# A batch-norm convolution kernel: rows of the transformed input padded from 342 to 344 columns, and both short blocks kept in one tile

## The chip, the cores and the metric

One core of a Trainium2 chip runs the whole kernel. The metric is the device time of one execution in microseconds (us), lower is better. The time before is 182.66 us, the median of three runs (182.33 to 183.10). One execution was profiled; its own time is 182.38 us.

## The reference: what is computed

`x` is 2 x 2048 x 1024 (item, position, input channel), `w` is 3 x 1024 x 1024 (tap, input channel, output channel), all bf16. A convolution over positions with three taps is followed by batch norm and SiLU:

```python
xp = jnp.pad(x, ((0, 0), (1, 1), (0, 0)))
y = sum(jnp.einsum('bsc,cd->bsd', xp[:, k:k + S, :], w[k]) for k in range(3))
y = (y - mean) * (g * 1.0 / jnp.sqrt(var + 1e-5)) + b
return silu(y)
```

## The kernel before, in words

The convolution is done in the Winograd manner: six neighbouring outputs are made from eight transformed inputs (`NJ = 8` points, `R = 6`). The 2048 positions of an item make 342 tiles of six (`NTILES`). A column tile is 128 input channels (`CT = 8`), an output tile 128 output channels (`DC = 8`).

**Input transform (the first 36 us).** A window holds 128 positions and gives 21 tiles (`WT`). For each item `bi` and column tile `ct` there are 16 windows. One matmul per window (line 225) multiplies it with a small matrix `rm` and leaves 8 x 21 = 168 values per channel in PSUM. A *job* (`Jobs.do`, line 220) is up to six such matmuls into two PSUM banks and one copy ("cast", line 240, executed at 242 on ScalarE, `a`, or 244 on VectorE, `d`) that writes them as bf16 into `T_sb[bi][:, ct, :, f*WT:...]`: 8 rows (one per point), in each a run of 126 or 84 columns. Three jobs (6, 6 and 4 windows; 128x1008, 128x1008 and 128x672 elements) fill a column tile. The last 6 of the 342 tiles of each item come from a *short block* (`do_short`, line 229): 48 rows of x, eight matmuls of 48 columns (line 233) and one cast that writes 6 columns into all 64 rows of `T_sb[bi]`. So `T_sb[bi]` is 128 partitions x 8 column tiles x 8 points x 342 columns.

**The order** is written by hand for every engine. `ORDER` (line 28) lists it: a letter names the pair of PSUM banks of a job (A: 4 and 5, B: 6 and 7, C: 2 and 3, D: 0 and 1), the small letter behind it the engine of the cast, `s2d` and `s4d` are the two short blocks, `z5` five idle matmuls, a number so many matmuls of the first product unit (`First`, line 391), which runs between the jobs. The framework adds the waits between engines: a reader waits for its writer, and an instruction that writes a place waits for whatever it sees as touching the same place before. PE, VectorE (DVE) and ScalarE (ACT) each work strictly in their order.

**Loads.** Everything is loaded by the SP queue in program order (lines 515 to 529), two half tiles by the ACT queue. The x tiles have six buffers (`XBUFS`), so from the seventh on a load waits until PE is done with an earlier one. `load_small` (line 88) takes the one buffer of `xlpool`, twice in turn.

**Products.** A product unit (output tile `dc`, item `bi`) runs eight products, one per point j; each is eight matmuls over the column tiles, with `T_sb[bi][:, ct, j, :]` (342 columns) as the moving operand (line 272; 391 for the first unit, whose item is 0). VectorE and ScalarE combine the eight results into six outputs and apply SiLU; POOL prepares the transformed weights of later output tiles. The last unit is cut into two halves of 214 and 128 columns (`Half`).

The lines that the change touches: 72 (allocation of `T_sb`), 86 to 91 (`load_small`), 229 to 238 (`do_short`).

Of the kernel before, what the change touches and what calls it, by code (L numbers as in the profile page):

```python
# [10 lines left out]
BF16 = mybir.dt.bfloat16  # L11
ENG = mybir.EngineType

P = 128
R = 6
NJ = 8
WT = 21
XBUFS = 6
LROWS = 48
NTILES = 342  # L20
NBP = 384


# [11 lines left out]
def kernel(  # L35
# [9 lines left out]
    nc = tc.nc  # L45
    B, CT, _, NF, _ = x.shape
    DC = w.shape[0]
    NB = NTILES
    LAST = NB - NF * WT
# [4 lines left out]
    tpool = ctx.enter_context(tc.tile_pool(name="tpool", bufs=1))  # L54
# [10 lines left out]
    xlpool = xscope.enter_context(tc.tile_pool(name="xlpool", bufs=1))  # L65
# [3 lines left out]
    )  # L69

    ps = pspool.tile([P, 8, 512], FP32, name="ps")
    T_sb = [tpool.tile([P, CT, NJ, NB], BF16, name=f"T_sb{bi}") for bi in range(B)]


    rm = consts.tile([P, NJ, WT], BF16, name="rm")
# [7 lines left out]
    dummy = consts.tile([P, 2], FP32, name="dummy")  # L83
    nc.vector.memset(dummy, 0.0)

    xt, raw, small = {}, {}, {}

    def load_small(bi):
        t = xlpool.tile([P, CT * P], BF16, name="xl")
        nc.sync.dma_start(out=t[0:LROWS], in_=xl[bi])  # L90
        small[bi] = t

    def load_x(bi, ct, parts=1):
        t = xpool.tile([P, NF, P], BF16, name="xw")
# [118 lines left out]
    class Jobs:  # L213
# [15 lines left out]
        def do_short(self, bank, eng):  # L229
            bi = self.short.pop(0)  # L230
            src = ps[:, bank, 0:CT * NJ * LAST].rearrange("p (c j n) -> p c j n", j=NJ, n=LAST)
            for c in range(CT):
                nc.tensor.matmul(  # L233
                    src[:, c], lhsT=small[bi][0:LROWS, c * P:(c + 1) * P], rhs=rm[0:LROWS, :, 0:LAST],
                    start=True, stop=True,
                )
            dst = T_sb[bi][:, :, :, NT:NB].rearrange("p c j n -> p (c j) n")
            self.out(dst, src.rearrange("p c j n -> p (c j) n"), eng)
# [11 lines left out]

    yts = [ypool.tile([P, R, NBP], BF16, name=f"yT{q}") for q in range(B)]
    half = [(H, NBP, ypool.tile([P, R, NBP - H], BF16, name="yh0")), (0, H, ypool.tile([P, R, H], BF16, name="yh1"))]
    for t, n in [(t, NB) for t in yts] + [(half[0][2], NB - H)]:
# [183 lines left out]
    class Half(Unit):  # L437


        def __init__(self, dc, bi, b0, q):  # L440
# [3 lines left out]
            n = hi - lo  # L444
            at = q * R * (NBP - H)
            self.to = out[bi, dc, :, at:at + R * n].rearrange("p (i n) -> p i n", i=R)
# [69 lines left out]
    load_x(0, 1, 2)  # L516
    nc.sync.dma_start(out=prm, in_=prm_in)
    load_small(0)
    scales()
    nc.scalar.activation(dummy[:, 1:2], dummy[:, 0:1], ACT.Silu)  # L520
    for ct in range(2, CT):
        load_x(0, ct)
        if ct == 2:
            load_w(0, (0, 2))
    load_w(0, (1,))
    load_small(1)
    for ct in range(CT):
        load_x(1, ct)
# [55 lines left out]
    dc, bi = seq[-1]  # L584
# [13 lines left out]

_OUTS = [((2, 8, 128, R * NBP), "bfloat16")]

# [12 lines left out]
def _laid_out(np, x, w, mean, var, g, b):  # L613
# [12 lines left out]
    for n in range(WT):  # L626
        rm[R * n:R * n + NJ, :, n] = np.array(_POINTS, np.float32).T
    return (
        wins,
        xp[:, step * NF:step * NF + LROWS],  # L630
        w.reshape(K, CT, P, DC, P).transpose(3, 2, 0, 1, 4),
# [33 lines left out]
```

## Time and profile before

| what | us |
|---|---|
| median of three runs | 182.66 |
| the profiled execution's own time | 182.38 |
| its span (first to last instruction) | 180.6 |
| PE busy | 173.9 (96%) |
| DVE, ACT, POOL busy | 150.8, 108.8, 139.5 |
| granted TensorE clock | 0.999 |
| DMA moved | 24.58 MB, mean 136 GB/s |

The span is divided by engine; a busy PE is one with a matmul in flight. The times of rows are counted from the start of the span. The 1.8 us between span and time lie outside the instructions.

### The profile page before, as it was taken

How to read it: one execution, taken by the hardware profiler on the slowest of the kernel's cores; microseconds unless marked ns; L12 is line 12 of the kernel's file. 1: busy time of each engine (PE TensorE's matmuls, PEld its weight loads, DVE VectorE, ACT ScalarE, POOL GpSimd, SP SyncE). 2: the span in 40 equal slices, each digit the busy share in tenths (PEclk: the TensorE clock that was granted, in tenths of full speed). 3: DMA queues.
4: the chain of work that ended last, by engine and by line, in shares of the span. 5: the costliest groups of instructions: out<-in, count | busy, mean ns of one | idle time of the engine just before them, and what ended most of it. 6: DMA issues, size and time to landing. Idle time of an engine off the chain costs nothing.

```text
span 180.6 us, 3487 instructions
## 1 busy us (share of the span) xinstructions
PE 173.9 (96%) x1372; PEld 124.8 (69%) x1372; DVE 150.8 (84%) x194; ACT 108.8 (60%) x173; POOL 139.5 (77%) x77
## 2 busy tenths in 40 slices
PE   7989899999999999999999999999999999999991
PEld 5878788866666666666666666666666666668890
DVE  0589778997969999999999999997978987766691
ACT  3777779968365756356545653555456454563773
POOL 2599999999997889999999999799799959000000
PEclk9999999999999999999999999999999999999999
DMA  5999992080316030723063305430303030203033
GB/s 173 368 416 378 409 414 109 16 333 5 132 59 250 0 131 0 195 115 131 0 169 139 131 0 127 182 131 2 127 7 131 0 120 16 97 34 127 7 160 103
DMA packets 7344, 24.58 MB, mean 136 GB/s; under 512 B 1088, under 2 KB 1600, under 8 KB 7328
## 3 DMA queue, kind: packets, MB, share of 16 engines
q1 hardware_dynamic: 6752, 23.74, 35.6%
q10 hardware_dynamic: 576, 0.63, 1.0%
q8 instruction: 10, 0.16, 0.4%
q14 instruction: 6, 0.05, 0.1%
HBM read 14.93 MB, written 9.44 MB: 135 GB/s over the span
## 4 chain that ended last, share of the span: by engine, by line
PE 86%; DMA 8%; DVE 3%; ACT 2%; issue 0%; ACTq 0%; DVEq 0%
PE ps L272 74%; DMA xw<-in_x_dram 8%; PE ps L225 6%; PE ps L391 4%; DVE ps L287 2%; ACT T_sb L242 1%; DVE t L287 1%; ACT yh L291 1%; PE ps L545 0%; ACTq L76 0%; DVEq L654 0%; PE ps L233 0%; DVE sd L287 0%; PE ps L588 0%; DVEq L287 0%
## 5 line engine op out<-in xcount | busy, mean ns | idle before, releaser
L272 PE MATMUL ps<-T_sb,u 128*128 128x342 bf16 (+2 forms) x768 | 109.4, 298 | 0.0
L272 PEld LDWEIGHTS <-u 128*128 128x128 bf16 x768 | 72.2, 97 | 32.6
L144 POOL TENSOR_TENSOR u<-e,w1x 128x1024 bf16<-128x1024 f32 x32 | 69.4, 2195 | 7.6 <-DVE e L137 6.3
L272 PE MATMUL ps<-T_sb,wch 128*128 128x342 bf16 (+2 forms) x256 | 39.5, 299 | 0.4 <-DVE ps L287 0.4
L287 DVE SCALAR_TENSOR_TENSOR t<-ps,sd 128x684 f32<-128x684 f32 (+2 forms) x49 | 37.6, 819 | 0.5
L144 POOL TENSOR_TENSOR u<-e,wch 128x1024 bf16<-128x1024 f32 x16 | 36.5, 2302 | 0.5
L291 ACT ACTIVATE yT<-ps,beta,scale 128x342 bf16<-128x342 f32 (+1 forms) x42 | 29.1, 727 | 12.6 <-PE ps L272 12.6
L272 PEld LDWEIGHTS <-wch 128*128 128x128 bf16 x256 | 24.2, 97 | 11.1 <-issue 0.5
L281 ACT COPY pc<-ps 128x342 f32<-128x342 f32 (+2 forms) x32 | 13.6, 424 | 28.2 <-PE ps L272 25.5
L242 ACT CAST T_sb<-ps 128x1008 bf16<-128x1008 f32 (+1 forms) x30 | 25.3, 883 | 6.7 <-PE ps L225 6.2
L244 DVE CAST T_sb<-ps 128x1008 bf16<-128x1008 f32 (+2 forms) x20 | 21.1, 1086 | 9.2 <-PE ps L225 8.3
L287 DVE SCALAR_TENSOR_TENSOR ps<-ps,t 128x684 f32<-128x684 f32 (+2 forms) x32 | 26.5, 829 | 0.7
L137 DVE SCALAR_TENSOR_TENSOR e<-wch 128x1024 f32<-128x1024 bf16 x12 | 26.3, 2188 | 0.0
L287 DVE SCALAR_TENSOR_TENSOR ps<-ps,pc 128x342 f32<-128x342 f32 (+2 forms) x34 | 16.9, 496 | 9.8 <-PE ps L272 7.0
L225 PE MATMUL ps<-rm,xw 128*128 128x168 bf16 x256 | 23.5, 242 | 1.6 <-DMA xw<-in_x_dram 0.7
L225 PEld LDWEIGHTS <-xw 128*128 128x128 bf16 x256 | 20.2, 100 | 4.8 <-DMA xw<-in_x_dram 2.8
L131 POOL TENSOR_TENSOR e<-wch 128x1024 f32<-128x1024 bf16 x8 | 19.0, 2378 | 0.3 <-DMA wch<-in_w_dram 0.3
L291 ACT ACTIVATE yT<-t,beta,scale 128x684 bf16<-128x684 f32 x15 | 14.4, 959 | 0.0
L287 DVE SCALAR_TENSOR_TENSOR t<-ps,t 128x684 f32<-128x684 f32 (+2 forms) x17 | 13.9, 817 | 0.0
L281 ACT COPY sd<-ps 128x342 f32<-128x342 f32 (+2 forms) x16 | 6.8, 426 | 10.3 <-PE ps L272 8.6
L283 ACT ACTIVATE pc<-ps 128x342 f32<-128x342 f32 (+2 forms) x16 | 7.0, 438 | 8.8 <-PE ps L272 6.1
L287 DVE SCALAR_TENSOR_TENSOR sd<-pc,ps 128x342 f32<-128x342 f32 (+2 forms) x17 | 8.2, 481 | 4.9 <-ACT sd L281 4.9
(44 smaller groups left out, 66.5 us busy)
## 6 DMA issues: line engine op xcount, KB each, us to landing
out_dram<-yT SPq DMA_DIRECT2D x15, 576.0 KB, 3.1
xw<-in_x_dram SPq DMA_DIRECT2D x14, 512.0 KB, 7.5
wch<-in_w_dram SPq DMA_DIRECT2D x7, 768.0 KB, 5.5
wch<-in_w_dram SPq DMA_DIRECT2D x3, 256.0 KB, 4.9
xw<-in_x_dram SPq DMA_DIRECT2D x2, 256.0 KB, 3.5
xw<-in_x_dram ACTq DMA_DIRECT2D x2, 256.0 KB, 4.4
out_dram<-yh SPq DMA_DIRECT2D x1, 256.0 KB, 2.0
xl<-in_xl_dram SPq DMA_DIRECT2D x2, 96.0 KB, 7.1
```

Of the source, the lines that this page charges most:

```text
L131: nc.gpsimd.tensor_tensor(sums[dc, q], a, b, op=ALU.add)
L137: nc.vector.scalar_tensor_tensor(out=e, in0=f, scalar=4.0, in1=h, op0=ALU.mult, op1=ALU.add)
L144: nc.gpsimd.tensor_tensor(wts[dc, q][:, i], sums[dc, q], o, op=(ALU.add, ALU.subtract)[i])
L225: nc.tensor.matmul(src[:, q // per, q % per], lhsT=xt[bi, ct][:, f + q], rhs=rm, start=True, stop=True)
L242: nc.scalar.copy(dst, src)
L244: nc.vector.tensor_copy(dst, src)
L272: nc.tensor.matmul(self.bank[q], lhsT=lhsT, rhs=T_sb[self.bi][:, ct, j, nsl], start=not add and ct == 0, stop=ct == CT - 1, skip_group_che ...
L281: nc.scalar.copy(dst, self.bank[q])
L283: nc.scalar.mul(dst, self.bank[q], by)
L287: nc.vector.scalar_tensor_tensor(out=out, in0=in0, scalar=scalar, in1=in1, op0=ALU.mult, op1=op1)
L291: nc.scalar.activation(self.yT[:, rows, self.y0:self.y0 + self.hi - self.lo], src, ACT.Silu, bias=beta[:, dc:dc + 1], scale=scale[:, dc:dc ...
L391: nc.tensor.matmul(self.bank[q], lhsT=lhsT, rhs=T_sb[self.bi][:, ct, j, :], start=not add and ct == 0, stop=ct == CT - 1, skip_group_check ...
```

## The change

- `T_sb[bi]` is allocated with 344 columns per row (`NBT`), and the name `T_sb[bi]` is bound to the slice of its first 342 columns, not to the tile itself. A row is then 688 bytes, not 684.
- The two short blocks share one tile `small`, which VectorE sets to zero once at the start. The first block is loaded to rows 0 to 47, as before; the second to rows 66 to 113.
- The second short block's eight matmuls go over all 128 rows of `small`, with the columns 11 to 16 of `rm` (whose entries for tile n stand in the rows 6n to 6n+7, zero elsewhere) instead of columns 0 to 5.

```diff
+SROW = 66
 NTILES = 342
+NBT = 344
...
-    T_sb = [tpool.tile([P, CT, NJ, NB], BF16, name=f"T_sb{bi}") for bi in range(B)]
+    T_sb = [tpool.tile([P, CT, NJ, NBT], BF16, name=f"T_sb{bi}")[:, :, :, 0:NB] for bi in range(B)]
...
-    xt, raw, small = {}, {}, {}
+    xt, raw = {}, {}
+    small = xlpool.tile([P, CT * P], BF16, name="xl")
+    nc.vector.memset(small, 0.0)
     def load_small(bi):
-        t = xlpool.tile([P, CT * P], BF16, name="xl")
-        nc.sync.dma_start(out=t[0:LROWS], in_=xl[bi])
-        small[bi] = t
+        nc.sync.dma_start(out=small[bi * SROW:bi * SROW + LROWS], in_=xl[bi])
...
+            rows, n = (slice(0, P), SROW // R) if bi else (slice(0, LROWS), 0)
             for c in range(CT):
                 nc.tensor.matmul(
-                    src[:, c], lhsT=small[bi][0:LROWS, c * P:(c + 1) * P], rhs=rm[0:LROWS, :, 0:LAST],
+                    src[:, c], lhsT=small[rows, c * P:(c + 1) * P], rhs=rm[rows, :, n:n + LAST],
                     start=True, stop=True,
                 )
```

## The prediction

> **What bounds the kernel now.** I read the chain of waits in order of time first, then the casts by shape, then who waited for whom, then the starts of single records, and last the wait lists of the two built programs.
>
> ```profile
> 6.21 1.91 ACT T_sb L242 x2
> ...
> 9.93 9.37 DMA xw<-in_x_dram
> 19.30 0.05 issue
> 19.35 1.04 PE ps L225 x12
> ...
> 33.73 0.44 PE ps L225 x6
> 34.17 0.14 PE ps L391
> 34.31 0.29 PE ps L225 x4
> 34.60 1.31 PE ps L391 x9
> ...
> 38.24 126.55 PE ps L272 x872
> ```
>
> From 19.35 us to 171.6 us the chain never leaves PE. Whatever stops PE in the transform of the second item (19.3 to 36 us) is therefore paid in full at the end, and whatever shortens a product matmul is gained in full. Before 19.3 us there is slack: PE waited there for the first x tile of the second item (issued 9.93, landed 19.30).
>
> ```profile
> L242 ACT CAST T_sb<-ps 128x1008 bf16<-128x1008 f32 x17 | 16.7, 1001 | 5.5 <-PE ps L225 5.1
> ...
> L242 ACT CAST T_sb<-ps 128x672 bf16<-128x672 f32 x13 | 9.5, 729 | 1.1 <-PE ps L225 1.1
> ...
> L244 DVE CAST T_sb<-ps 128x1008 bf16<-128x1008 f32 x15 | 17.8, 1205 | 3.2 <-PE ps L225 2.8
> ...
> L244 DVE CAST T_sb<-ps 128x672 bf16<-128x672 f32 x3 | 2.6, 851 | 5.5 <-PE ps L225 5.5
> ...
> L244 DVE CAST T_sb<-ps 128x384 bf16<-128x384 f32 x2 | 1.1, 550 | 0.5 <-PE ps L233 0.5
> ```
>
> The casts wait for matmuls (L225, L233) and for nothing else that shows, so the two engines fill one column tile side by side. In the second item ScalarE's first casts of successive column tiles start at 28.12, 29.86 and 31.60 us: **1.74 us per column tile**, which is ScalarE's own 1.00 + 0.73.
>
> ```profile
> PE ps L225 <- DVE T_sb L244: 0.6, 1, 0.6
> ...
> PE ps L225 <- ACT T_sb L242: 0.2, 1, 0.2
> ```
>
> These two rows, from the table of waits, say that PE hardly waits for a cast today, 0.8 us in all.
>
> **Part 1, the padding as a layout.** In the 126 us product stretch I took the starts of single matmul records, within groups of eight of the same point j, twelve units each. Mean distance: j=0 and 4: 144.75 and 144.62 ns; j=3 and 7: 144.82 and 144.77; j=2 and 6: 145.08 and 145.32; j=1 and 5: 145.63 and 145.69. A row of point j starts 684j bytes into its block, which modulo 16 is 0, 4, 8 and 12 for these four pairs. With 688 bytes all start at 0. If all then run like the first pair (144.68 against a mean of 145.09), the gain is 0.40 ns x some 1,000 matmuls = **0.4 us**. Bounds: 0 (the distances follow j for another reason) to 1.0 us (all at the shortest single distance seen often, 144 ns). I take 0.4, as the order by the remainder holds in all four pairs. The Trainium skill bears on this from two sides. "SBUF — State Buffer" (Specifications) says that SBUF has 16-byte lines and that each cross to a new line costs; a 684-byte row touches 43 lines from remainder 0 or 4 and 44 from 8 or 12, and the trace agrees, with the two slower pairs 0.3 to 1.0 ns behind. "TensorE: Matmul & The Clock Gate" (Wait — 56ns, not 53.3ns?) gives columns / 2.4 + 2.5 ns whatever the address, so 145.0 ns, by which the gain would be 0.1 us.
>
> **Part 2, the padding as a program.** `T_sb[bi]` becomes a slice of a tile, and in the wait lists the casts have changed. Before, casts into one column tile had no wait for each other (a "126" of VectorE waited for PE and an old ScalarE cast of another tile). Now every cast of a column tile waits for the one before it in the same tile, on whichever engine that ran. The first item's short cast waits for the VectorE cast before it, and the next column tile's first cast waits for it. The data do not overlap, but the program makes them a chain. Links: a semaphore comes 10 ns after the end, and the released engine starts 23 ns later (measured on VectorE after ScalarE), so 0.03 us; where the wait stands in a separate semaphore instruction ahead (as with ScalarE after VectorE in the new lists), its row of 21 ns and 44 ns more come on top, 0.09 us; a next cast on the same engine without a wait starts 0.1 us before the last ends.
>
> *Second item.* Column tiles 2, 3 and 5 are ScalarE 6 windows, VectorE 6, ScalarE 4, the others alike: 1.00 + 0.03 + 1.21 + 0.09 + 0.73 - 0.10 = **2.96 us** per tile, against 1.74. ScalarE is first and last, so the next tile cannot start early. PE needs 16 x 0.073 + 4 x 0.145 = 1.75 us per tile and is no longer the bound.
>
> *First item,* with the same durations: second cast of tile 0 at 6.21 (as now), first of tile 1 at 7.11, VectorE's cast of tile 1 8.14 to 9.35, short 9.38 to 9.93, tile 2 VectorE 9.96 to 11.17, ScalarE 11.26 to 12.26. Then VectorE's 4-window cast of tile 2 to 13.14, tile 3 VectorE 13.19 to 14.40, tile 4 VectorE to 15.53, ScalarE 15.62 to 16.62 and 16.65 to 17.38. Tile 5's ScalarE cast waits for a VectorE cast that PE releases late (17.45 to 18.45). Tile 6: ScalarE to 19.35, VectorE 19.38 to 20.59. Tile 7: VectorE 20.65 to 21.86 (PE five products late) and 21.89 to 23.10, ScalarE 23.19 to 23.92. The second item's first cast starts at 23.8 us, against 19.99 now: **3.8 us late**, of which the old wait at 19.3 hides nothing, since 23.8 lies behind it.
>
> *Where PE meets it.* From 23.8: tile 0 to 1 takes 2.96 + 0.35 (one more ScalarE copy, L400, stands between), six more tiles 6 x 2.96. Tile 7's first cast starts at 44.9, so tile 6's last cast ends at 45.0. That cast frees banks 6 and 7 for tile 7's six matmuls that start at 33.73 now: 45.04, **11.3 us late**. Behind them PE has the same work in the same order. Tile 7's own casts are then three on ScalarE, 1.00 + 0.03 + 1.00 + 0.03 + 0.73, ending at 47.7; the first product that reads tile 7 comes at 45.04 + (34.60 - 33.73) + 1.31 + 7 x 0.145 = 48.2, so it just does not wait. From there PE is again the bound to the end.
>
> **Part 3, the short blocks.** The zeroing is 512 elements of 32 bits in the built program. The row for 256 such elements takes 0.27 us, so 0.54: 1.12 to 1.66 us on VectorE, whose next work begins at 6.62 now. The first `load_small`, which now waits for it, is issued at 2.09: nothing. The Trainium skill, "VectorE: DVE Perf Modes" (Zero memsets can be issued as uint32), names this rewriting; as 1024 bf16 elements it would be 1.07 us by its rule, to 2.19, and SP's queue would slip by 0.1 us, still hidden by SP's later waits. The second load no longer waits for the first short block's matmuls; these end at 8.07 and the load goes at 8.67, behind another issue: nothing. The eight matmuls over 128 rows: the weight load of 48 rows takes 93 ns, of 128 rows 98 (L225), so between 0 and, at L225's pace of 73 ns instead of 40, 8 x 0.033 = 0.3 us; I take 0, the row of weight loads being the nearest, and PE waits around them anyway. Later x loads are issued when PE frees their buffers, up to 4 us later than now, but the queue holds about 9 us of loads (9.93 to 19.30) and each tile is wanted later too: nothing.
>
> **Sum.** +11.3 - 0.4 = +10.9. The profiled execution took 182.38 us (span 180.6 and 1.8 outside): **193.3 us**; it lies 0.28 under the median shown, well inside its spread.
>
> **Rivals.**
> - *A, the forecast: 193.3* (own range 191.3 to 195.2: fifty links at plus or minus 0.03 us are 1.5, the bounds of parts 1 and 3 are +0.7 and -0.6).
> - *B, the first item's delay is absorbed: 189.5.* If its chain overlaps better than I drew it and is through by 19.3, the second item starts at 19.99 as now and only its own stretch counts: 11.3 - 3.8 - 0.4 = +7.1. For it: PE and DMA have slack there. Against: tile 2 alone starts 0.7 late and tile 7 has two VectorE casts in a row.
> - *C, not slower: 182.0.* The place is the handover between the casts of one tile. If the waits are met by the time they are asked, the period stays 1.74 and only the 0.4 us of padding is left. It decides at the point where the other engine's cast ends before this one's matmuls do. Against: 1.00 + 1.21 + 0.73 is already 2.94 without any link.
> - *D, the clock falls: 196.5.* PE would stand still 1.2 us in each 2.96. Granted clock is now 1.00 with single stops of 0.88 us. Were it halved, a tile's PE work would be 3.5 us, 0.55 over the chain, six tiles: +3.2. Against: no single stop would reach 2 us. The Trainium skill, "TensorE: Matmul & The Clock Gate" (Why this matters for your kernels), asks for no idle gaps over about 3 us, by which D would not come; no row here shows such a gap.
>
> **How the numbers follow.** A 0.85, B 0.06, C 0.05, D 0.04. The range 190.8 to 195.4 holds nearly all of A. A measurement of this kernel can tell about 0.5% (0.9 us) from no change. A, B and D are slower; C is within 0.5%, with 0.01 left for more gain from the padding: faster 0.01, same 0.04, slower 0.95.
>
> **What would show it.** Right: PE's L225 waits for casts (the two rows above) grow from 0.8 to some 13 us; ScalarE's first casts in the second item 2.9 to 3.0 us apart; the last L225 at 45 us; single matmul distances alike for all j at 144.7. Wrong: casts of one tile overlapping in time; a period near 1.74; stops of PE after 48 us; a clock under 0.97.

## The result and the profile after

The changed kernel took **194.32 us** (median of five runs, 194.16 to 194.89) against 182.60 for the kernel before on the same chip (five runs, 182.25 to 183.10): ratio 1.065, 95% interval 1.0626 to 1.0674. The forecast was 193.3. The profiled execution took 194.16 us, its span is 192.4 (before 182.38 and 180.6), 11.8 us more. The lines have moved by five or six in this kernel: the transform's matmul is now at 230, the short block's at 239, the casts at 248 (ScalarE) and 250 (VectorE), the products at 278 and 397.

The chain of waits in order of time (start, us, what), from tile 6 of the second item to the products:

```profile
41.76 0.73 ACT T_sb L248
...
42.53 0.90 PE ps L230 x10
43.43 1.20 DVE T_sb L250
...
44.71 0.73 ACT T_sb L248
...
45.48 0.59 PE ps L230 x6
...
50.14 126.44 PE ps L278 x872
```

In the kernel before, this stretch of the chain was PE alone. Now it passes through ScalarE and VectorE for each column tile, and PE takes it over for good at 45.48 us. The ten PE matmuls that the view puts ahead of VectorE's cast are not what released it: in the single records VectorE's wait for PE is over by 43.19, ScalarE's first cast of the tile ends at 43.38, and VectorE's cast starts at 43.415, 0.03 us later. Further ahead, the same view goes from ScalarE (32.91) to VectorE (34.57) directly.

PE did the same six matmuls for tile 7 before. The chain shows them at 33.73 there, but a piece of the chain begins only where the record of the piece before it ends, and PE starts its next matmul earlier than that. The time lines of PE, before and after, give their own starts:

```profile
33.57 0.60 PE L225 MATMUL ps<-rm,xw 128*128 128x168 bf16 x6
```

```profile
45.48 0.59 PE L230 MATMUL ps<-rm,xw 128*128 128x168 bf16 x6 [0.91 <-ACT T_sb L248]
```

So they come **11.9 us late**, and so does the product stretch behind them: it begins at 50.14 instead of 38.24 and lasts 126.44 instead of 126.55 us.

The casts by shape, busy us and mean ns of one, then the idle time before them and what ended it, ScalarE's first:

```profile
L248 ACT CAST T_sb<-ps 128x1008 bf16<-128x1008 f32 x17 | 16.8, 1002 | 3.5 <-DVE T_sb L250 1.7 <-PE ps L230 1.6
L248 ACT CAST T_sb<-ps 128x672 bf16<-128x672 f32 x13 | 9.3, 718 | 15.3 <-DVE T_sb L250 13.9 <-PE ps L230 1.3
```

```profile
L250 DVE CAST T_sb<-ps 128x1008 bf16<-128x1008 f32 x15 | 18.0, 1207 | 11.0 <-PE ps L230 6.3 <-ACT T_sb L248 4.3
L250 DVE CAST T_sb<-ps 128x672 bf16<-128x672 f32 x3 | 2.6, 857 | 7.9 <-ACT T_sb L248 7.9
```

A single cast costs what it cost before (1002 and 1207 ns against 1001 and 1205). New are the releasers: casts of one engine now wait for casts of the other, in both directions. The table of waits sums it up (us, times, longest):

```profile
ACT T_sb L248 <- DVE T_sb L250: 15.6, 12, 2.0
...
DVE T_sb L250 <- ACT T_sb L248: 12.2, 6, 5.7
...
PE ps L230 <- ACT T_sb L248: 9.0, 13, 1.2
...
PE ps L230 <- DVE T_sb L250: 1.0, 2, 0.7
```

The first two rows did not exist before; the last two stood at 0.2 and 0.6. Of VectorE's 12.2 us, 5.7 are the wait ahead of its first cast, which before was 5.5 us of waiting for PE.

ScalarE's time line in the second item (start, us; the idle time ahead in brackets). Each row is the last cast of one column tile and the first of the next, back to back:

```profile
32.91 1.62 ACT L248 CAST T_sb<-ps 128x672 bf16<-128x672 f32 x2 [1.33 <-DVE T_sb L250]
35.86 1.62 ACT L248 CAST T_sb<-ps 128x672 bf16<-128x672 f32 x2 [1.33 <-DVE T_sb L250]
```

The rows follow each other by 2.95 us: 1.62 us of work and 1.33 us in which ScalarE waits for VectorE's one cast (1.20) and the two handovers around it.

### The profile page after: what moved, and what is told of

Same layout as the page of the kernel before. It is cut to its first block, busy times and chain, and to the rows that moved or that the text cites. A ratio compares the mean times of both kernels' runs of the same rounds, so it can differ in the third digit from the quotient of the medians.

```text
span 192.4 us, 3504 instructions
## 1 busy us (share of the span) xinstructions
PE 176.2 (92%) x1372; PEld 126.2 (66%) x1372; DVE 149.6 (78%) x195; ACT 108.7 (57%) x173; POOL 139.6 (73%) x77
## 4 chain that ended last, share of the span: by engine, by line
PE 76%; DVE 11%; ACT 8%; DMA 2%; issue 1%; DVEq 0%; ACTq 0%
PE ps L278 70%; DVE T_sb L250 9%; ACT T_sb L248 7%; PE ps L230 4%; PE ps L397 2%; DMA rm<-in_rm_dram 2%; DVE ps L293 1%; DVE t L293 1%; ACT yh L297 1%; PE ps L551 0%; PE ps L239 0%; ACT kept L406 0%; DVEq L660 0%; DVE sd L293 0%; ACTq L248 0%
## 5 line engine op out<-in xcount | busy, mean ns | idle before, releaser
L250 DVE CAST T_sb<-ps 128x1008 bf16<-128x1008 f32 (+2 forms) x20 | 21.7, 1089 | 19.1 <-ACT T_sb L248 12.2
L230 PE MATMUL ps<-rm,xw 128*128 128x168 bf16 x256 | 24.8, 242 | 10.4 <-ACT T_sb L248 9.0
L230 PEld LDWEIGHTS <-xw 128*128 128x128 bf16 x256 | 20.7, 100 | 15.5 <-issue 13.4
L142 DVE SCALAR_TENSOR_TENSOR e<-wch 128x1024 f32<-128x1024 bf16 x12 | 23.8, 1980 | 0.0
L136 POOL TENSOR_TENSOR e<-w1x,wch 128x1024 f32<-128x1024 bf16 x4 | 8.5, 2125 | 9.7 <-ACT w1x L126 9.6
```

The lines of the kernel that those rows point to most:

```text
L136: nc.gpsimd.tensor_tensor(sums[dc, q], a, b, op=ALU.add)
L142: nc.vector.scalar_tensor_tensor(out=e, in0=f, scalar=4.0, in1=h, op0=ALU.mult, op1=ALU.add)
L230: nc.tensor.matmul(src[:, q // per, q % per], lhsT=xt[bi, ct][:, f + q], rhs=rm, start=True, stop=True)
L250: nc.vector.tensor_copy(dst, src)
```

## The experiments

Eight kernels were run in two groups. The kernel before gave 182.61 us beside the first four (182.19 to 183.71) and 182.77 beside the others (182.24 to 183.49).

### short_only: the short blocks' part alone

Against the changed kernel:

```diff
-NBT = 344
+NBT = 342
...
-    T_sb = [tpool.tile([P, CT, NJ, NBT], BF16, name=f"T_sb{bi}")[:, :, :, 0:NB] for bi in range(B)]
+    T_sb = [tpool.tile([P, CT, NJ, NBT], BF16, name=f"T_sb{bi}") for bi in range(B)]
```

> The change with rows of 342 columns again (one tile for both short blocks, its zeroing and the 128-row matmuls stay). Chain theory: the waits between casts are gone from the wait list, so the time of before, 182.6 us, within 0.3; ScalarE's first casts in the second item 1.74 us apart. Rival, the short blocks cost (zeroing delays SP's loads, 128-row matmuls, the second block's load): some of the 11.7 us stays, 183.5 us or more.

Measured: 182.38 us (182.05 to 183.56), ratio 0.9992 [0.9971, 1.0014]. The product stretch starts and lasts as before, within 0.1 us:

```profile
38.15 126.55 PE ps L278 x872
```

The zeroing, the shared tile and the matmuls over 128 rows cost nothing that can be measured. The whole loss lies in the other line of the change.

### pad_only: the padding alone, without a slice under the name

Against the kernel before; the name stays bound to the whole tile, and the first unit's products read the 342 columns by an explicit range:

```diff
+NBT = 344
-    T_sb = [tpool.tile([P, CT, NJ, NB], BF16, name=f"T_sb{bi}") for bi in range(B)]
+    T_sb = [tpool.tile([P, CT, NJ, NBT], BF16, name=f"T_sb{bi}") for bi in range(B)]
...
-                self.bank[q], lhsT=lhsT, rhs=T_sb[self.bi][:, ct, j, :],
+                self.bank[q], lhsT=lhsT, rhs=T_sb[self.bi][:, ct, j, 0:NB],
```

> The kernel before with rows of 344 columns, T_sb bound to the whole tile (readers cut to 342 columns), the short blocks as before. Chain theory: the wait list has the chain, so 194.3 us, within 0.4, and a period of 2.95 us. Rival, it was the short blocks or the binding to a slice: 182.6 us.

Measured: 194.62 us (194.0 to 194.96), ratio 1.0654 [1.0626, 1.0683]; ScalarE's first casts start at 31.01, 33.95, 36.90, 39.85 and 42.80 us, 2.95 apart. From the waits and the chain:

```profile
PE ps L226 <- ACT T_sb L243: 9.2, 13, 1.2
```

```profile
50.56 126.44 PE ps L273 x872
```

The padded row length is enough for the whole loss; the slice is not needed for it.

### slice_only: the slice without the padding

Against the kernel before:

```diff
-    T_sb = [tpool.tile([P, CT, NJ, NB], BF16, name=f"T_sb{bi}") for bi in range(B)]
+    T_sb = [tpool.tile([P, CT, NJ, NB], BF16, name=f"T_sb{bi}")[:, :, :, 0:NB] for bi in range(B)]
```

> The kernel before with T_sb bound to a slice that is the whole tile (342 of 342 columns). Chain theory: no chain in the wait list, so 182.6 us, within 0.3. Rival, the slice makes the waits: 194.3.

Measured: 182.32 us (182.07 to 183.59), ratio 0.9993 [0.9972, 1.0014]; the product stretch starts at 37.92 us. Binding the name to a slice makes no chain. The forecast's part 2 opens with the slice as if it belonged to the cause; it does not.

### pitch_343: rows one column longer

Against the changed kernel. Its wait list has no waits between the casts of one tile, so that a padded row stands here without the chain:

```diff
-NBT = 344
+NBT = 343
```

> The change with 343 columns per row instead of 344; the wait list of this program has no chain. Chain theory: padding as such costs nothing, so 182.6 us, within 0.5, period 1.74. Rival, padded rows are slow in themselves (casts that write with gaps): about 194. Row starts are then 686j bytes, remainders 0, 14, 12, 10, 8, 6, 4, 2 modulo 16: if the start within 16 bytes sets the pace of a matmul, the distances of single matmuls differ by j by 0.5 to 1 ns, as in before; if the mean pace is set elsewhere, each j has 145.0 to 145.1 on the mean.

Measured: 182.85 us (182.5 to 183.91), ratio 1.0021 [1.0001, 1.0042]. ScalarE's time line and the chain:

```profile
24.52 11.32 ACT L248 CAST T_sb<-ps 128x1008 bf16<-128x1008 f32 x13 [0.77 <-PE ps L230]
```

```profile
38.21 126.89 PE ps L278 x872
```

Thirteen casts follow each other without a stop, and the period is 1.74 us again. So padding as such does not cost 11.7 us; the waits that the program gets with 344 do. The price that is left is another one: the 872 matmuls take 126.89 instead of 126.55 us. Rows now start at all even remainders of 16 bytes, and the mean distances for j = 0 to 7 are 145.0, 146.19, 145.80, 146.08, 145.07, 145.63, 145.05 and 145.77 ns, 145.57 over all. So they do depend on where the row starts: remainders 0, 8 and 4 (j = 0, 4 and 6) stand at 145.0 to 145.1, the other five at 145.6 to 146.2.

### pad_second_item and pad_first_item: the chain in one item alone

Against the changed kernel, with `(344, 342)` in place of `(342, 344)` for the other of the two:

```diff
-NBT = 344
+NBT = (342, 344)
...
-    T_sb = [tpool.tile([P, CT, NJ, NBT], BF16, name=f"T_sb{bi}")[:, :, :, 0:NB] for bi in range(B)]
+    T_sb = [tpool.tile([P, CT, NJ, NBT[bi]], BF16, name=f"T_sb{bi}")[:, :, :, 0:NB] for bi in range(B)]
```

> The change with 344 columns for the second item's T_sb alone, 342 for the first's. Chain theory: the first item runs as before, its last cast ends near 19.7, the second item's casts start near 20.0 and go 2.95 us apart: 194.3 less the first item's share of 3.8 to 4.3, so 190.0 to 190.5 us. Rival, the first item's delay was absorbed in any case and all of it is the second's: 194.3.

> The change with 344 columns for the first item's T_sb alone. Chain theory: the second item starts 3.8 to 4.3 us late and then keeps its 1.74 us per column tile: 186.4 to 186.9 us. Rival, slack of PE and DMA before 19.3 us absorbs the first item's chain: 182.6.

Measured: second item alone 190.02 us (189.87 to 190.28), ratio 1.0383 [1.0353, 1.0414], +7.25; first item alone 186.76 (186.72 to 187.83), ratio 1.0222 [1.0185, 1.0259], +3.99. The chain where PE resumes, and where the products start, of the second item alone and then of the first alone:

```profile
41.51 0.60 PE ps L230 x6
...
46.17 126.53 PE ps L278 x872
```

```profile
24.36 0.60 PE ps L230 x6
...
42.60 126.53 PE ps L278 x872
```

```profile
28.93 11.30 ACT L248 CAST T_sb<-ps 128x1008 bf16<-128x1008 f32 x13 [0.77 <-PE ps L230]
```

With the first item alone padded, the second starts some 4 us late and then runs at its old pace (the last line, ScalarE without a stop). With the second alone padded, its first cast comes at 20.34 us, near the 19.99 of before, and the next follow 2.95 us apart. The two add up to 11.24 us, against 11.7 for both; by the starts of the product stretch they add up to 12.29, against 11.90, so the sum holds within half a microsecond. The first item's delay is not absorbed; that it would be was rival B.

### after_scalar_casts and before_scalar_casts: one engine for the second item's casts

If a chain of handovers sets the period, three ScalarE casts per column tile must be faster than ScalarE, VectorE, ScalarE, although VectorE then stands nearly idle; without the chain they must be slower. The edit moves VectorE's cast of the second item's column tiles 1 to 6 to ScalarE (tile 7 is ScalarE's alone already). The same edit of `ORDER` was made in the changed kernel and in the kernel before:

```diff
-    "3 Aa Cd Ba 7 s4d Ca Bd Aa 4 Ca 1 Bd Aa 3 Ca 2 Ad Ba 2 Ca 2 Bd Aa 2 Ca 2 Ad Ba 2 Ca 3 Ba 1 Aa 1"
+    "3 Aa Ca Ba 7 s4d Ca Ba Aa 4 Ca 1 Ba Aa 3 Ca 2 Aa Ba 2 Ca 2 Ba Aa 2 Ca 2 Aa Ba 2 Ca 3 Ba 1 Aa 1"
```

> The change with all casts of the second item's column tiles 1 to 7 on ScalarE (letters in the order alone; the short block's cast stays on VectorE). Chain theory: handing a tile to VectorE and back gains nothing under the chain, 1.00 + 0.03 + 1.00 + 0.03 + 0.73 - 0.10 = 2.69 us per tile against 2.95, so six tiles give 1.6: 192.7 us, faster though VectorE does no such cast. Rival, the engines' own casts are the bound (contention, slower writes): taking one engine away costs, over 196.

> The kernel before with the same letters: second item's tiles 1 to 7 cast by ScalarE alone. Without a chain ScalarE needs 0.90 + 0.90 + 0.62 = 2.42 us per tile against 1.74, so slower here, by 3 to 4.5 us: 185.6 to 187.1. So the same edit helps with the chain and hurts without it. Rival, the edit helps in both: under 182.6.

Measured: in the changed kernel 192.77 us (192.49 to 192.92), ratio to the kernel before 1.0535 [1.0508, 1.0562], 1.5 us less than the changed kernel (1.7 when each is counted from the kernel before as measured beside it); ScalarE's first casts are 2.68 us apart. In the kernel before 185.97 (185.59 to 186.78), ratio 1.0171 [1.0135, 1.0206], 3.2 us more; period 2.39. The chain of the first and the waits of the second:

```profile
41.99 0.99 ACT T_sb L248
...
43.01 0.73 ACT T_sb L248
...
43.78 0.59 PE ps L230 x6
```

```profile
PE ps L225 <- ACT T_sb L242: 2.3, 5, 0.6
```

One edit helps where the casts are chained and hurts where they are not. That tells the chain apart from any cause that slows PE or the casts themselves: it is the order of the casts of one tile that binds. Between two chained ScalarE casts there is a gap of some 0.03 us (42.98 to 43.01), so that a cast starts 1.03 to 1.04 us after the one that it waits for; unchained 6-window casts start 0.89 us after each other. Two such links in each column tile make up the difference between the periods, 2.68 and 2.39.

## Why the prediction was right

**Part 2, the chain.** It is the whole result: pad_only has all of the loss, short_only and slice_only none, and pitch_343 has a padded row without the chain and stays within 0.4 us of before. The period was forecast at 2.96 us and measured at 2.95, tile 0 to 1 of the second item at 3.31 and 3.29 (24.30 to 27.59). In the first item the order and the releaser of every cast came as drawn; the times slip slowly. These are the pieces of the changed kernel's chain from its beginning:

```profile
6.30 1.01 ACT T_sb L248
...
9.60 0.57 DVE T_sb L250
10.26 1.22 DVE T_sb L250
11.56 1.91 ACT T_sb L248 x2
13.49 1.22 DVE T_sb L250
...
21.07 1.22 DVE T_sb L250
22.39 1.22 DVE T_sb L250
23.68 1.63 ACT T_sb L248 x2
```

Drawn were 6.21 for the first piece, 9.38 and 9.96 for the VectorE casts, 11.26, 13.19, 20.65, 21.89 and 23.19 for the later ones. The slip is 0.1 at the first and 0.15 at the first cast of tile 1 (7.26 instead of 7.11; the first cast of all starts at 5.22 instead of 4.98, since `rm` landed at 4.14 instead of 3.90), 0.22 at 9.60, 0.30 at 10.26, 0.42 at 21.07 and 0.5 at 22.39. In three of these steps a VectorE cast follows a VectorE cast: from 9.495 to 9.598, 10.156 to 10.26 and 22.282 to 22.386, **0.10 us each where 0.03 was put down**. By the wait lists each of the three waits for VectorE and for PE, and the wait for VectorE stands in a separate semaphore instruction ahead of the cast; the chain shows it for the second:

```profile
10.17 0.03 issue
10.20 0.02 DVEq L250
```

For this case the forecast had 0.09 in its own list of links and used it only for ScalarE after VectorE. (For the first of the three the chain names PE's matmuls that end at 9.59 instead, but they are another job's; the short block's own matmuls end at 8.62.) Three times 0.07 and the 0.15 of the start are 0.36 of the 0.5; the step of 0.1 ahead of 21.07 lies in PE's own work before it and was not taken apart. ScalarE to VectorE was right: in all thirteen places VectorE's cast starts 32 to 33 ns after the end of the ScalarE cast.

**Where PE meets it.** PE resumes at 45.48, forecast 45.04; the first cast of tile 7 is at 45.33, forecast 44.9. The casts of tile 7 end at 48.11, and no stop of PE behind them shows, as drawn. The forecast counted its 11.3 us from 33.73, where the chain shows the six matmuls in the kernel before; they start at 33.57 (the time line above), so its own drawing gives 11.47. That is 0.16 more in the sum.

The same overlap of matmuls explains a sign that came out smaller than named. PE's waits for casts are 10.0 us in the two rows (10.7 with the rows of two other lines, 397 and 239), not "some 13". Up to its resumption PE stood idle 9.5 us longer than before. The record of a matmul of 168 columns lasts 0.236 us, while the next one starts 0.072 us behind it, so at each stop the last 0.16 us still count as busy. Fifteen stops at 0.16 are 2.4 us, and 9.5 + 2.4 are the 11.9 us by which PE is late. The matmuls themselves are not slower after a stop: the six from 45.48 start 71 to 72 ns apart, the six from 33.57 72 to 73.

**Part 1, the alignment, is the term that was mis-sized.** The forecast took 0.4 us. The product stretch fell by 0.11 us (126.55 to 126.44). No run has rows of 344 columns in both items without the chain, so this is read from the stretch and not timed by itself. The step that failed is "if all then run like the first pair". With every row at remainder 0 all eight points stand at 145.0 ns, not at 144.7; in the changed kernel each of the 893 distances between neighbouring product matmuls of 342 columns reads 145 ns. In the kernel before, the mean over all points is 145.1, and within a group of eight some steps have a mean of 144.1 to 144.3 ns and others of 147 to 148. The aligned points have none of the long steps, and their short ones come first in the group, behind another point's; that they make up there for time lost by their neighbours fits the trace but was not tested. So the measurement decides for the smaller of the two gains named. The Trainium skill, "TensorE: Matmul & The Clock Gate" (Wait — 56ns, not 53.3ns?), whose formula has no term for the address, gives 342 / 2.4 + 2.5 = 145.0 ns as an estimate, and that agrees with the trace of the 688-byte rows to the last digit shown. The count of 16-byte lines, which the forecast took from the Trainium skill, "SBUF — State Buffer" (Specifications), puts the points of the 684-byte rows in order, but not those of the 686-byte rows of pitch_343: j=4 touches 44 lines and has 145.07 ns, j=7 touches 43 and has 145.77. So it is not shown that crossing lines is what costs the 0.1 ns.

**Part 3.** It cost nothing, as forecast. The zeroing runs ahead of everything that needs it, in the span's first two microseconds, and the load behind it is issued at 2.08 against 2.09 before:

```profile
1.18 0.48 DVE L93 MEMSET xl<- 128x512 uint32 x1
```

Two times the row of 256 elements gave 0.54 us; it took 0.485. The second load goes at 8.97 instead of 8.67; short_only has it at 9.01 and loses nothing by it. The matmuls of the second short block take 188 to 193 ns against 183 to 185 for the first, and start 25 to 30 ns apart in both; the weight loads take 92 to 93 ns for 48 rows and 96 to 100 for 128.

**The sum.** 11.3 - 0.4 was forecast. Measured: 11.3 + 0.16 (the start of the six matmuls before, read too late) + 0.44 (the slip of the casts) - 0.11 (the alignment) = 11.8. All three corrections go the same way and none hid another; together they are the 0.9 us by which the forecast was low. The terms of the forecast's own range add up to 191.2 to 195.5, a little wider than written; the measured time lies in both.

**The rivals.** B (189.5) fell with pad_first_item: its delay of 3.99 us is paid in full. The 7.1 that B gave the second item alone was measured as 7.25. C (182.0) fell with the period. D (196.5) did not come: the granted clock has a mean of 0.996, and the page's row of it, in tenths by 40 slices of the span, is full through the stops, of which the longest is 1.2 us (all in the first ten slices):

```profile
PEclk9999999999999999999999999999999999999998
```

The single stops of 0.88 us that D gives for the kernel before stand in no row; PE's longest wait for a cast there is 0.6 us by the table of waits.

**What stays open.** Why the program gets the waits at a row of 344 columns (also, by the wait lists, at 346) and not at 342 or 343 was not settled; the casts write the same columns in all of them. Nor was it settled what makes the matmuls of the 684- and 686-byte rows slower by 0.1 and 0.6 ns.

## What to carry to other kernels

When only a layout changes, compare the wait lists of the two programs before thinking about addresses: an innocent row length can turn instructions that ran side by side into a chain, and a chain costs its period minus that of the old bound, times the number of tiles, wherever the bound engine is the one that waits in the end. Look at both engines' releasers: two engines that each wait for the other are the sign of it, and giving all links to one engine is a quick test. In a chain view, a piece of an engine whose instructions overlap begins where the record before it ends; take the start of the single record before adding to it. A gain that is read from differences between neighbouring matmuls should be taken from the mean of all of them, not from the fast half.

## What the runs showed of the hardware

- Matmuls with 342 moving columns came every 145.0 ns with 688-byte rows, every 145.1 in the mean with 684-byte rows and every 145.57 with 686-byte rows; the product stretch of 872 of them took 0.34 us longer with the last than with 684.
- A cast whose wait for another cast stood in a separate semaphore instruction ahead of it started 0.09 (ScalarE after VectorE) to 0.10 us (VectorE after VectorE) after the other's end. Where that wait stood on the cast itself, it was 0.03 us (VectorE after ScalarE, and ScalarE after ScalarE).
- After a stop of 0.9 us PE's next six matmuls of 168 columns started 71 to 72 ns apart, 72 to 73 without the stop, with the clock granted in full.
